# Banded attention into a squared-ReLU MLP: the last quarter of W1 in two column halves, the first loads in another order, one group's gate moved

## The chip, the cores and the metric

One core of a Trainium2 chip runs the whole program; seven cores are not used. The metric is the device time of one execution in microseconds (us), lower is better. The time before is the median of three runs. A profile is one further execution, recorded by the hardware; its span is the stretch from the first to the last recorded instruction, a little less than the device time of that same execution.

The engines go by short names: PE (matrix multiply), PEld (its weight load), DVE (vector), ACT (scalar, activation), POOL (GpSimd), SP (sync). Each runs its own instructions strictly in the order in which they were written into its stream; an instruction that waits on a semaphore holds up everything behind it on that engine. Transfers are started by POOL, SP and ACT and are carried out by 16 shared DMA engines.

## The reference

```python
# q, k, v: [8 batches, 8 heads, 576 tokens, 64], float32
scores = (q @ k.T) / sqrt(64);  only |query - key| <= 32 is kept
attn   = softmax(scores);       x = attn @ v
x      = x as [8*576 = 4608 tokens, 8*64 = 512]
h      = x @ w_in               # w_in  (W1): 512 x 2048
g      = relu(h) ** 2
out    = g @ w_out              # w_out (W2): 2048 x 512
```

## The kernel before, in words

**Groups.** The 4608 tokens are cut into 24 groups G of 192 query tokens, three to a batch (b, g = G // 3, G % 3). A group has two key windows of 128 keys, w = 0 ("A") and w = 1 ("B"). The program names its steps, and the texts below use the same names:

- `turnk`, `turnq` (L485): for the first two batches, G < 6, PE transposes the rows of k and q into `kt` and `qt`; the result is evicted from PSUM by DVE (k, L516) or ACT (q, L513). Later groups are turned by DMA transposes from SP (L524).
- S (L565) scores of a group, X (L586 for group 0, L589 for the rest) the exponential on ACT, M (L594) the band mask on DVE. For group 0 the mask is added in PSUM as a bias (L548), so it has no M.
- P (L613, L617, L622) attention times v, with a column of ones that gives the row sums; R (L641) the reciprocal, N (L644) the normalisation into `xa` (64 tokens) and `xb` (128 tokens), Z (L650) a memset of part of the PSUM tile between PA and PB.
- T and XT: x is transposed into `xt`, by PE and evictions for G < 3 (L666, L671, L696, L701; L675, L685, L688, L713), by DMA transposes from SP afterwards (L717, L720).
- A (`mm1`, L737): x times W1, in blocks of 192, later 256 and 512 tokens. At 192 tokens one piece covers two of the sixteen 128-column strips d of W1, that is eight matmuls; the eight pieces of the first block are A0.0, A0.2, ... A0.14. Then Relu on ACT (L743) and the square on DVE (L746) into `gt`.
- B (`mm2`, L757): 128 tokens times W2, four matmuls for each quarter of W2, then an eviction on ACT (L767) and a store. The last 128 tokens go through `mm2_last` (L782).

**Loads.** k, q and v of the first groups, W1 and W2 are loaded by POOL (the transfers convert float32 to bfloat16). k and q of group 0 come instead through SP as float32 into the output buffer `oe` (`load_hw`, L407) and are cast by ACT and DVE (L414, L417). For groups 1 to 5, `load_pair` (L426) loads k or q into a pair buffer `PR[t][G % NPR]`, and a DVE copy (L429) sorts the pairs into `raw`; with three such buffers groups 4 and 5 use those of groups 1 and 2 again, so their POOL transfer waits for the earlier copy. W1 comes in four quarters of 512 columns (`load_w1`, L456), each with a semaphore of its own; piece A.d waits for quarter d // 4. W2 comes in four quarters of 512 rows (L461). `copy_v` (L450) copies 64 rows of one v tile to the next instead of loading them twice.

**Order.** The table `OPENING` gives the order of the first transfers: entry number n gets the priority `K + n` with K = -100, and POOL issues in this order. All other work has a key that grows with the group or the token block. `Prog.rec` notes every operation with what it reads and writes, an estimated duration and its key. `Prog.schedule` is a list planner: whenever an engine is free in the planner's own clock, it takes the ready operation with the least key. It has a small model of the DMA queues (`move`, `slack`, `LANDQ`), so the planned landing of a load decides where its consumers stand in each engine's stream. `Prog.emit` writes the streams in the planned order, with semaphore waits for what is not ordered already. The planner's times have no effect on the chip except through this order. Where PE would stand idle before the second transpose of group 0's `xb`, the planner fills the gap with matmuls on zeros ("idle", L322) that nothing reads.

**The gate.** Loads from group 6 on (`load_qk`, L394, and `load_v`, L443) carry an extra dependency from `gate(G)`: for G below `GFAR` the A piece or score that was recorded last at that point (`self.moe`), from `GFAR` on the step PB of group G - 3. POOL waits for it before it issues the load. The key of these loads is 3G - 13 - 9, from `GFAR` on 3G - 13 - 8.5.

Of the kernel before, what the change touches and what calls it, by code (L numbers as in the profile page):

```python
# [22 lines left out]
LEAD = 13.0  # L23
LAG = 9.0
AHEAD = 9.0
GFAR = 9
GATE = 'P{}B'
GD = 3
GK = 8.5
# [3 lines left out]
HMOVE = 27  # L33
PMOVE = 20
WMOVE = 81
VMOVE = 14.5
TISS = 1340
TMOVE = 15
NVR = 24
VKEY = 10.0  # L40
TSLACK = 3500
XSLACK = 2500
LSLACK = 3000
NCLR = 1
LANDQ = 2000
PQ = 100
VCS = 6
NDUP = 1
NPR = 3
LSLACK1 = 1000  # L50
HOLD = {}
KMIN = 0.5
HOLDT = 26000
KSPL = 0
XTD = 1
NSPLIT = 3
HWB = 150
# [8 lines left out]
VSET = (-9.8, -6.8)  # L66
ESPLIT = 0
IOTA = -1
OPENING = [("k", 1), ("w1", 0), ("v", 0, 0), ("v", 1, 1), ("q", 1), ("v", 0, 1), ("q", 2), ("k", 2), ("v", 1, 0), ("w1", 1),
           ("w1", 2), ("w1", 3), ("q", 5), ("v", 2, 0), ("v", 2, 1), ("w2", 1), ("k", 3), ("v", 3, 0), ("q", 3), ("w2", 0), ("w2",  # L70
           2), ("k", 4), ("v", 3, 1), ("q", 4), ("v", 5, 0), ("v", 5, 1), ("w2", 3), ("hq", 0), ("k", 5), ("v", 4, 0), ("v", 4, 1),
           ("hk", 0)]
WARM = 40000
LAST = ((0, 256), (256, 384), (384, 512))
KC = ((0, 224), (224, 192), (416, 160))
# [204 lines left out]
class Gen:  # L280
# [5 lines left out]
    def alloc(self):  # L286
# [24 lines left out]
        self.OEB = sb("oe", [128, 4, 512], F32)  # L311
        self.PR = {t: [sb(f"{t}pair{i}", [128, 1024], BF16) for i in range(NPR)] for t in "qk"}
        self.BIAS = [sb(f"bias{i}", [128, 128], BF16) for i in range(4)]
# [67 lines left out]
    def gate(self, G):  # L381
        if G < 6:
            return None
        return self.p.named[GATE.format(G - GD)] if G >= GFAR else self.moe

# [33 lines left out]
    def load_pair(self, t, b, g, key):  # L419
# [3 lines left out]
        G = 3 * b + g  # L423
        pr, raw = self.PR[t][G % NPR], self.RAW[t][G % NRAW]
        s = (self.q if t == "q" else self.k)[b][:, t0:t0 + n, :].rearrange("h (p r) d -> p h (r d)", r=2)
# [8 lines left out]
    def load_v(self, b, g, key, js=(0, 1)):  # L434
        G = 3 * b + g
        vt = self.V[G % NV]
        for j in js:
            k0 = 192 * g - 32 + 128 * j
            lo, hi = max(k0, 0), min(k0 + 128, S_)
            if g and j == 0 and G < NVR:  # L440
# [3 lines left out]
                vt[lo - k0:hi - k0, j, :, 0:64], self.v[b, :, lo:hi, :].rearrange("h p d -> p h d")),  # L444
                writes=[("v", G % NV, j)], dma=(f"v{G % NV}{j}", G), key=key, dur=500 + 3 * n, move=(n // 2, VMOVE),
                name=f"v{b}{g}{j}", after=self.gate(3 * b + g), slack=LSLACK if b > 1 else LSLACK1 * b)
# [4 lines left out]
                   reads=[("v", (G - 1) % NV, 1)], writes=[("vl", G % NV)], key=key + VKEY, dur=300, name=f"vc{G}",  # L451
                   after=self.moe if G >= VCS else None)

    def load_w1(self, d, key):
        src = self.w_in[:, 512 * d:512 * d + 512].rearrange("(f p) c -> p f c", p=128)
        self.p.rec("POOL", lambda e: e.dma_start(self.W1[:, :, 512 * d:512 * d + 512], src),  # L456
                   writes=[("w1", d)], dma=(f"w1{d}", 0), key=key, dur=770, move=(32, WMOVE), name=f"w1{d}")

    def load_w2(self, d, key):
        src = self.w_out[512 * d:512 * d + 512, :].rearrange("(k p) c -> p k c", p=128)  # L460
        self.p.rec("POOL", lambda e: e.dma_start(self.W2[:, 4 * d:4 * d + 4, :], src),  # L461
                   writes=[("w2", d)], dma=(f"w2{d}", 0), key=key, dur=770, move=(32, WMOVE), name=f"w2{d}")

# [8 lines left out]
    def turn_pe(self, t, b, g, key):  # L472
# [32 lines left out]
        w = (t + "t", b % 2, g)  # L505
        if t == "k" and G == 0 and KSPL:
            for x, (c0, c1) in enumerate(((0, KSPL), (KSPL, h))):
# [144 lines left out]
    def xturn(self, G):  # L652
# [4 lines left out]
        if G < NXT:  # L657
# [48 lines left out]
            if two:  # L706
                for x, (c0, c1) in enumerate(((0, 64), (64, 192))):
# [10 lines left out]
                   reads=[("xa", G % 3)], writes=wr[:1], dma=(f"xa{G % 3}", G), key=key - 0.5 + XKEY[0], dur=TISS, move=(16, TMOVE), name=f"T{G}a",  # L718
                   slack=XSLACK)
        self.p.rec("SP", lambda e: e.dma_start(self.XT[:, :, r + 64:r + 192], xb[:], transpose=True),  # L720
                   reads=[("xb", G % 3)], writes=wr[1:], dma=(f"xb{G % 3}", G), key=key - 0.5 + XKEY[1], dur=TISS, move=(32, TMOVE), name=f"T{G}b", slack=XSLACK)

    def mm1(self, t0, n, ds, key):
        k = self.k1
        self.k1 += 1
        ht, rt, gt = self.HT[k % 2], self.RT[k % 4], self.GT
        r = t0 % RING
        c = n * len(ds)  # L730
        d0 = ds[0]
        steps = [(t0 // 64 + x) % (RING // 64) for x in range(n // 64)]

        def f(e):
            for x, d in enumerate(ds):
                for ft in range(4):
                    mm = e.matmul(ht[:, n * x:n * x + n], self.W1[:, ft, 128 * d:128 * d + 128], self.XT[:, ft, r:r + n],  # L737
                                  start=(ft == 0), stop=(ft == 3))
            return mm

        self.moe = self.p.rec("PE", f, reads=[("xt", s) for s in steps] + [(("xt", s), 1) for s in steps if t0 < 192 and XTD] + [("w1", d0 // 4)], writes=[f"ht{k % 2}"], key=key,
                   dur=4 * len(ds) * max(n / 2.4 + 2.5, 33), name=f"A{t0}.{d0}")
        self.p.rec("ACT", lambda e: e.activation(rt[:, 0:c], ht[:, 0:c], ACTF.Relu), reads=[f"ht{k % 2}"],  # L743
                   writes=[("rt", k % 4)], key=key, dur=act(c), name=f"r{t0}.{d0}")
        rr = rt[:, 0:c].rearrange("p (d t) -> p d t", d=len(ds))
        self.p.rec("DVE", lambda e: e.tensor_tensor(gt[:, d0:d0 + len(ds), r:r + n], rr, rr, ALU.mult),  # L746
                   reads=[("rt", k % 4)], writes=[("gt", s, d) for s in steps for d in ds], key=key, dur=dve(c),
                   name=f"g{t0}.{d0}")
# [50 lines left out]
    def build(self):  # L799
        p = self.p  # L800
        self.k1 = 0
        self.moe = None
        K = -100.0
        self.setup_idle()
        self.setup_iota(K + IOTA)
        self.setup_id(K)
        self.setup_mask(2, K + 1)
        self.setup_bias(2, K + 1.1)
        self.setup_mask(1, K + 2)
        self.setup_bias(1, K + 2.1)  # L810
        self.setup_k(0, K + 0.5)
        self.setup_v(0, K + 1.5)
        self.setup_v(1, VSET[0])
        self.setup_v(2, VSET[1])
        self.setup_mask(0, MKEY[0])
        self.setup_mask(3, MKEY[1])
        for i in range(3, NV):
            self.setup_v(i, -9)
        self.setup_k(1, -9)
        for n, it in enumerate(self.opening()):  # L820
            kd, a = it[0], it[1:]
            key = K + n
            if kd == "w1":
                self.load_w1(a[0], key)
            elif kd == "w2":
                self.load_w2(a[0], key)
            elif kd == "v":
                self.load_v(*divmod(a[0], 3), key, a[1:])
            elif kd[0] == "h":
                self.load_hw(kd[1], a[0], key)  # L830
            else:
                self.load_pair(kd, *divmod(a[0], 3), key)
        for g in (1, 2, 4, 5):
            self.copy_v(g, K + 7 if g < 3 else 3 * g - LEAD - AHEAD)
        todo = []

        def at(key, f, *a):
            todo.append((key, len(todo), f, a))

        for G in range(NG):  # L840
            b, g = divmod(G, 3)
            if b > 1:
                key = 3 * G - LEAD - (GK if G >= GFAR else AHEAD)
                for t in "kq":
                    at(key, self.load_pair if G < NPAIR else self.load_qk, t, b, g, key)
                at(key, self.load_v, b, g, key)
                if g and G < NVR:
                    key = 3 * G - LEAD - 0.5 if G >= VCS else key
                    at(key + 0.01, self.copy_v, G, key - VKEY if G >= VCS else key)
            for t in "kq":  # L850
                key = 3 * G - LEAD - (0.6 if b < NTURN else TDKEY)
                at(key, self.turn_pe if b < NTURN else self.turn_dma, t, b, g, key)
            for ws in ((0,), (1,)) if G < NSPLIT else ((0, 1),):
                at(3 * G - LEAD + 0.3 * ws[0], self.scores, G, ws)
            for w in range(2):
                at(3 * G - LEAD + 0.3 * w + 0.1, self.pv, G, w)
            at(3 * G - LEAD + 0.5, self.xturn, G)
        t0 = 0
        while t0 < NTOK:
            n = FIRST[t0] if t0 in FIRST else 192 if t0 < 768 else 256 if t0 < T512 else 512  # L860
            m = min(512 // n, 4)
            for d in range(0, 16, m):
                key = t0 / 64 + d / 16 * n / 64
                at(key, self.mm1, t0, n, list(range(d, d + m)), key)
            t0 += n
        at(500, self.mm2_last, NBLK - 1, 500)
        for u in range(NBLK - 1):
            for seg in range(4):
                at(2 * u + LAG + seg * 0.5, self.mm2, u, seg, 2 * u + LAG + seg * 0.5)
        for key, _, f, a in sorted(todo, key=lambda x: x[:2]):  # L870
            f(*a)
        p.schedule()
        with self.nc.Block():
            dsems, dcount = p.emit()
            for s in dsems:
                if s[0] == "o":
                    self.nc.sync.wait_ge(dsems[s], dcount[s])
# [35 lines left out]
```

## Time and profile before

| | us |
|---|---|
| median of 3 runs (lowest to highest) | 302.03 (301.92 to 302.29) |
| profiled execution, device time | 301.87 |
| its span | 299.9 |
| PE busy in the span | 291.9 (97%) |
| DVE, ACT, POOL busy | 167.2, 160.3, 107.1 |
| first piece of x times W1 starts | 17.46 |
| last of the eight pieces of the first block starts to run, with the one before it | 24.11 |
| stores left after the last matmul | 297.58 to 299.9 |

The span can be read in three parts. Until 17.46 us PE does the transposes, scores and P V of the first groups, with zero matmuls between them. From there to about 297.6 us it is busy nearly without a gap. Then the last stores land. The granted PE clock is 1.00 throughout. The DMA engines are busy from 3 us to about 230 us.

### The profile page before, as it was taken

The page shows a single profiled execution, that of the slowest core. Times are in us where ns is not written, and L with a number is a line of the kernel's source. Part 1 is how long each engine was busy: PE and PEld are TensorE (multiplying, and loading weights), DVE is VectorE, ACT ScalarE, POOL GpSimd, SP SyncE. Part 2 cuts the span into 40 slices and gives each one's busy share as a digit, 9 for nine tenths or more (in the row PEclk, how much of TensorE's full clock was granted, in tenths as well). Part 3 has the DMA queues.
Part 4 walks back from the last instruction along what each step waited for, and adds up shares of the span by engine and source line. Part 5 has one row for each costly group of instructions (what it writes and reads, how often), then busy time and mean ns, then how long its engine had stood idle before and what let it go on. Part 6 is the DMA issues. An engine that isn't in the chain of part 4 may idle for free.

```text
span 299.9 us, 6209 instructions
## 1 busy us (share of the span) xinstructions
PE 291.9 (97%) x2394; PEld 171.8 (57%) x2431; DVE 167.2 (56%) x385; ACT 160.3 (53%) x250; POOL 107.1 (36%) x143
## 2 busy tenths in 40 slices
PE   7899999999999999999999999999999999999996
PEld 3578866848677767664544454444544444444445
DVE  6898775737674767563656666665666632222100
ACT  3497834836467656750765476536744643443312
POOL 8993336503544354455256335533500000000000
PEclk9999999999999999999999999999999999999999
DMA  9999999997999999999999999999992120100112
GB/s 169 176 206 184 196 177 174 169 176 137 164 169 165 95 162 146 155 138 186 180 168 131 114 166 156 125 149 156 154 128 70 55 61 35 37 35 35 38 70 105
DMA packets 160636, 39.83 MB, mean 133 GB/s; under 512 B 149984, under 2 KB 156128, under 8 KB 160608
## 3 DMA queue, kind: packets, MB, share of 16 engines
q0 software_dynamic: 106016, 17.93, 89.3%
q1 hardware_dynamic: 49264, 12.14, 28.5%
q10 hardware_dynamic: 5328, 9.37, 9.1%
q8 instruction: 19, 0.31, 0.5%
q14 instruction: 9, 0.07, 0.1%
HBM read 36.70 MB, written 9.44 MB: 154 GB/s over the span
## 4 chain that ended last, share of the span: by engine, by line
PE 90%; DMA 5%; POOL 3%; issue 1%; ACT 0%; POOLq 0%; ACTq 0%
PE ht L737 41%; PE outp L757 40%; DMA w<-in_moe_w_in_dram 5%; PE at L622 4%; PE at L565 4%; POOL v L443 1%; POOL w L456 1%; PE at L485 1%; PE ht L782 1%; PE outp L782 1%; POOL kpair L426 1%; POOL qpair L426 1%; ACT rt L743 0%; ACT oe L792 0%; POOL dif L325 0%
## 5 line engine op out<-in xcount | busy, mean ns | idle before, releaser
L737 PE MATMUL ht<-xt,w 128*128 128x256 bf16 (+2 forms) x885 | 140.0, 302 | 1.3 <-DMA w<-in_moe_w_in_dram 0.5
L757 PE MATMUL outp<-w,gt 128*128 128x512 bf16 x536 | 133.0, 379 | 1.3
L743 ACT ACTIVATE rt<-ht 128x512 bf16<-128x512 f32 (+1 forms) x152 | 85.9, 578 | 87.1 <-PE ht L737 85.1
L737 PEld LDWEIGHTS ht<-xt,w 128*128 128x128 bf16 x896 | 81.3, 98 | 43.8 <-ACT rt L743 0.6
L746 DVE TENSOR_TENSOR gt<-rt 128x512 bf16<-128x512 bf16 (+1 forms) x152 | 61.5, 408 | 61.6 <-ACT rt L743 60.0
L757 PEld LDWEIGHTS outp<-w,gt 128*128 128x128 bf16 x560 | 51.9, 98 | 54.1 <-ACT oe L767 1.0
L394 POOL DMA_DIRECT2D kraw<-in_k_dram x36 | 27.7, 778 | 107.3 <-PE at L622 56.8
L589 ACT ACTIVATE e<-at 128x1024 bf16<-128x1024 f32 x46 | 44.8, 1021 | 8.7 <-PE at L565 8.4
L594 DVE TENSOR_TENSOR pt<-e,mask 128x1024 bf16<-128x1024 bf16 x46 | 31.8, 691 | 29.0 <-ACT e L589 28.9
L443 POOL DMA_DIRECT2D v<-in_v_dram x48 | 38.2, 809 | 0.0
L767 ACT ACTIVATE oe<-outp 128x512 f32<-128x512 f32 x35 | 21.1, 604 | 29.6 <-PE outp L757 29.6
L394 POOL DMA_DIRECT2D qraw<-in_q_dram x36 | 27.7, 778 | 0.0
L622 PEld LDWEIGHTS at<-v,pt 128*128 128x128 bf16 x384 | 18.3, 98 | 9.9 <-DMA v<-in_v_dram 0.6
L622 PE MATMUL at<-v,pt 128*128 128x65 bf16 x384 | 20.1, 194 | 0.5 <-ACT pt L586 0.5
L644 DVE TENSOR_TENSOR xa<-at,rs 64x512 bf16<-64x512 f32 x24 | 16.7, 695 | 0.9
L644 DVE TENSOR_TENSOR xb<-at,rs 128x512 bf16<-128x512 f32 x24 | 16.5, 689 | 0.7
L565 PEld LDWEIGHTS at<-qt,kt 64*128 64x128 bf16 x384 | 10.8, 94 | 8.7 <-issue 7.1
L565 PE MATMUL at<-qt,kt 64*128 64x128 bf16 x384 | 15.2, 217 | 0.2
L641 DVE RECIPROCAL rs<-at 64x8 f32<-64x8 f32 (+1 forms) x48 | 10.0, 209 | 9.1 <-PE at L622 7.7
L650 DVE MEMSET at<- 64x520 f32 x23 | 11.3, 492 | 3.5 <-DVE xa L644 2.6
L450 DVE COPY v<-v 64x512 bf16<-64x512 bf16 x16 | 5.9, 372 | 5.1 <-PE ht L737 2.9
L789 DVE COPY oe<-ht 128x128 f32<-128x128 f32 x1 | 0.3, 292 | 14.5 <-PE ht L782 14.5
(67 smaller groups left out, 83.2 us busy)
## 6 DMA issues: line engine op xcount, KB each, us to landing
out_dram<-oe ACTq DMA_DIRECT2D x35, 256.0 KB, 3.2
qraw<-in_q_dram POOLq DMA_DIRECT2D x36, 96.0 KB, 5.8
w<-in_moe_w_in_dram POOLq DMA_DIRECT2D x4, 512.0 KB, 10.7
v<-in_v_dram POOLq DMA_DIRECT2D x16, 128.0 KB, 6.6
w<-in_moe_w_out_dram POOLq DMA_DIRECT2D x4, 512.0 KB, 18.8
v<-in_v_dram POOLq DMA_DIRECT2D x16, 96.0 KB, 7.0
kraw<-in_k_dram POOLq DMA_DIRECT2D x12, 112.0 KB, 4.6
kraw<-in_k_dram POOLq DMA_DIRECT2D x12, 96.0 KB, 4.9
```

Of the source, the lines that this page charges most:

```text
L394: self.p.rec("POOL", lambda e, j=j: e.dma_start(raw[0:h, j, :].rearrange("p (h d) -> p h d", h=8), s[:, j]), writes=[("raw", t, G % NRAW, ...
L443: self.p.rec("POOL", lambda e, j=j, lo=lo, hi=hi, k0=k0: e.dma_start(vt[lo - k0:hi - k0, j, :, 0:64], self.v[b, :, lo:hi, :].rearrange("h ...
L565: mm = e.matmul(sc[:, 512 * par + 128 * j:512 * par + 128 * j + 128], kt[r:r + 64, j, k0:k0 + 128], q, start=G >= NBIAS, stop=True, skip_g ...
L589: self.p.rec("ACT", lambda e, e_=e_, sc=sc: e.activation(e_[:], sc, ACTF.Exp, scale=0.125), reads=tags[w], writes=[("e", n % 2)], key=key, ...
L594: self.p.rec("DVE", lambda e, pt=pt, ee=ee, mb=mb: e.tensor_tensor(pt[:], ee, mb, ALU.mult), reads=[("e", n % 2), ("mask", mi)], writes=[( ...
L622: mm = e.matmul(avp[:, c:c + 65], pt[:, 4 * (h % 2) + h // 2, :], vt[:, w, h, 0:65], start=(w == 0 and y == 0), stop=True, skip_group_chec ...
L644: self.p.rec("DVE", lambda e: e.tensor_tensor(x[r0:128, :].rearrange("p (x y c) -> p x y c", x=2, y=4), av[:, :, :, 0:64], rb, ALU.mult), ...
L737: mm = e.matmul(ht[:, n * x:n * x + n], self.W1[:, ft, 128 * d:128 * d + 128], self.XT[:, ft, r:r + n], start=(ft == 0), stop=(ft == 3))
L743: self.p.rec("ACT", lambda e: e.activation(rt[:, 0:c], ht[:, 0:c], ACTF.Relu), reads=[f"ht{k % 2}"], writes=[("rt", k % 4)], key=key, dur= ...
L746: self.p.rec("DVE", lambda e: e.tensor_tensor(gt[:, d0:d0 + len(ds), r:r + n], rr, rr, ALU.mult), reads=[("rt", k % 4)], writes=[("gt", s, ...
L757: mm = e.matmul(op[:], gt[:, d, r:r + 128], self.W2[:, d, :], start=(d == 0), stop=(d == 15))
L767: self.p.rec("ACT", lambda e: e.activation(oe, op[:], ACTF.Copy), reads=[f"outp{u % 2}"], writes=[("oe", u % 4)], key=key, dur=act(512), n ...
```

## The change

1. `load_w1` takes an optional half. The last quarter of W1 is loaded as two transfers of 256 columns, each with its own semaphore; a piece of `mm1` waits only for the half that it reads. The other three quarters are loaded as before, under two names.
2. `OPENING` has a new order. q of group 2 is POOL's first transfer, in place of k of group 1; v of group 0 comes next; the first quarter of W1 moves from second to seventh place; the order behind W1 changes too.
3. `KSPL` goes from 0 to 48: the eviction of group 0's transposed k (L516) is done in two instructions, the first with keys 0 to 95, so that the scores of window A of group 0 wait only for the first. The code for this is in the kernel already.
4. `NPR` goes from 3 to 4: a fourth pair buffer each for k and q.
5. `GFAR` goes from 9 to 10: group 9's loads are gated by `self.moe` and have the key 5 in place of 5.5.
6. `XSLACK` goes from 2500 to 3000: the planner counts 0.5 us more until a DMA transpose of x has landed.

```diff
-GFAR = 9
+GFAR = 10
 WMOVE = 81
+WHALF = 43
-XSLACK = 2500
+XSLACK = 3000
-NPR = 3
+NPR = 4
-KSPL = 0
+KSPL = 48
-OPENING = [("k", 1), ("w1", 0), ("v", 0, 0), ("v", 1, 1), ("q", 1), ("v", 0, 1), ("q", 2), ("k", 2), ("v", 1, 0), ("w1", 1),
-           ("w1", 2), ("w1", 3), ("q", 5), ("v", 2, 0), ("v", 2, 1), ("w2", 1), ("k", 3), ("v", 3, 0), ("q", 3), ("w2", 0), ("w2",
-           2), ("k", 4), ("v", 3, 1), ("q", 4), ("v", 5, 0), ("v", 5, 1), ("w2", 3), ("hq", 0), ("k", 5), ("v", 4, 0), ("v", 4, 1),
-           ("hk", 0)]
+OPENING = [("q", 2), ("hq", 0), ("v", 0, 0), ("v", 0, 1), ("hk", 0), ("v", 1, 1), ("k", 1), ("q", 1), ("w1", 0), ("k", 2), ("v",
+           1, 0), ("w1", 1), ("w1", 2), ("w1", 3, 0), ("w1", 3, 1), ("v", 2, 0), ("v", 2, 1), ("w2", 0), ("k", 3), ("q", 3), ("v",
+           3, 1), ("q", 5), ("w2", 1), ("v", 5, 1), ("v", 3, 0), ("w2", 2), ("k", 4), ("q", 4), ("w2", 3), ("v", 4, 1), ("k", 5),
+           ("v", 4, 0), ("v", 5, 0)]
-    def load_w1(self, d, key):
-        src = self.w_in[:, 512 * d:512 * d + 512].rearrange("(f p) c -> p f c", p=128)
-        self.p.rec("POOL", lambda e: e.dma_start(self.W1[:, :, 512 * d:512 * d + 512], src),
-                   writes=[("w1", d)], dma=(f"w1{d}", 0), key=key, dur=770, move=(32, WMOVE), name=f"w1{d}")
+    def load_w1(self, d, key, half=None):
+        c, n = (512 * d, 512) if half is None else (512 * d + 256 * half, 256)
+        src = self.w_in[:, c:c + n].rearrange("(f p) c -> p f c", p=128)
+        self.p.rec("POOL", lambda e: e.dma_start(self.W1[:, :, c:c + n], src),
+                   writes=[("w1", d, x) for x in ((0, 1) if half is None else (half,))], dma=(f"w1{c}", 0), key=key, dur=770,
+                   move=(32, WMOVE if half is None else WHALF), name=f"w1{d}" + ("" if half is None else f".{half}"))
...
-        self.moe = self.p.rec("PE", f, reads=[...] + [("w1", d0 // 4)], ...
+        self.moe = self.p.rec("PE", f, reads=[...] + [("w1", d0 // 4, x) for x in sorted({d // 2 % 2 for d in ds})], ...
...
             if kd == "w1":
-                self.load_w1(a[0], key)
+                self.load_w1(a[0], key, *a[1:])
```

More of the change, by code (lines that the diff above doesn't have):

```diff
@@ L739, in f @@
             return mm
-        self.moe = self.p.rec("PE", f, reads=[("xt", s) for s in steps] + [(("xt", s), 1) for s in steps if t0 < 192 and XTD] + [("w1", d0 // 4)], writes=[f"ht{k % 2}"], key=key,
+        self.moe = self.p.rec("PE", f, reads=[("xt", s) for s in steps] + [(("xt", s), 1) for s in steps if t0 < 192 and XTD] + [("w1", d0 // 4, x) for x in sorted({d // 2 % 2 for d in ds})], writes=[f"ht{k % 2}"], key=key,
                    dur=4 * len(ds) * max(n / 2.4 + 2.5, 33), name=f"A{t0}.{d0}")
```

## The prediction

> **What bounds the kernel now.** I read the page's chain of work that ended last first, then the same chain in order of time, then PE's waits and PE's timeline of the first 26 us, then the other engines and the landings there.
>
> ```profile
> PE 90%; DMA 5%; POOL 3%; issue 1%; ACT 0%; POOLq 0%; ACTq 0%
> ```
> ```profile
> 10.19 13.79 DMA w<-in_moe_w_in_dram
> 23.98 0.14 issue
> 24.11 1.48 PE ht L737 x16
> ```
>
> From 24.11 on the chain is PE. What starts it is the last quarter of W1: issued at 10.19, landed at 23.98. PE's waits of at least 0.2 us behind the first piece of x times W1 (17.46) are this one of 0.5 and two of 0.2. Windows of 50 us between 50 and 250 show PE busy for 49.53 to 49.63 us. So PE has a fixed amount of work after the opening, and the change can only move the moment from which it is packed, or open a hole later.
>
> ```profile
> 13.78 0.51 PE L485 MATMUL ht<-ident,qraw 96*128 96x96 bf16 x8 [0.17 <-DVE qraw L429]
> 14.13 0.42 PE L613 MATMUL at<-v,pt 128*128 128x65 bf16 x8
> 15.42 0.40 PE L565 MATMUL at<-qt,kt 64*128 64x128 bf16 x8
> 17.14 0.40 PE L565 MATMUL at<-qt,kt 64*128 64x128 bf16 x8
> 17.46 0.83 PE L737 MATMUL ht<-xt,w 128*128 128x192 bf16 x8
> ...
> 24.11 1.48 PE L737 MATMUL ht<-xt,w 128*128 128x192 bf16 x16 [0.47 <-DMA w<-in_moe_w_in_dram]
> 25.43 0.42 PE L622 MATMUL at<-v,pt 128*128 128x65 bf16 x8
> ```
>
> The columns are start, duration, what, and in brackets the idle time before and who ended it. The second window of group 0 (PB, 14.13) stands behind turnq1; scores S1A and S1B run at 15.42 and 17.14. The wait of 0.47 stands before A0.12 and A0.14, which need the last quarter; they end at 24.11 + 1.48 = 25.59. That is my reference point.
>
> Landings (issue plus time to landing): k1 7.3, W1.0 9.8, v00 10.5, v11 11.5, q1 12.4, v01 13.3, q2 14.4, k2 15.5, v10 15.7, W1.1 18.2, W1.2 21.3, W1.3 24.0. POOL had issued all of these by 11, so the order of issue and the width of the path set them, and the steps between them are prices: a W1 quarter 2.5 to 3.1, a q or k pair 0.9 to 1.1, a v tile 0.2 to 1.0.
>
> **The last quarter.** The twelve transfers up to W1.3 are the same ones as before, in another order, so the last byte lands where it did, about 24.0. The split adds one issue on POOL (0.77, L456; POOL runs ahead of the landings by 13, so nobody waits for it) and one more transfer. The trace has no half of a quarter. Nearest rows for the extra transfer: v10 landed 0.2 behind k2, so at most about 0.2 more; the quarters' steps of 2.5 to 3.1 leave 0.3 to gain. I take 0.1, the row of the small transfer being nearer: last half at 24.1, first half about 1.4 before it, 22.7. PE started 0.14 after the landing. Now one piece instead of two stands behind it, 1.48 / 2 = 0.74. End of the first block: 24.1 + 0.14 + 0.74 = 24.98, against 25.59: **-0.6**, with -1.0 and -0.5 as the bounds by landing alone. It holds only if PE has finished all else by 24.24.
>
> The Trainium skill, page "DMA: Bandwidth & Descriptors", section "Anatomy of one DMA — SWDGE (gpsimd) path", gives each such transfer a fixed cost of about 2.0 us and, in "Measured (HBM→SBUF, 128 partitions, SWDGE, issued from GpSimd)", advises batches of at least 1 MiB, which speaks against splitting a quarter that reads 1 MB. If that fixed cost added up in the queue, the sum would be 2 us worse; by the rows here transfers land 0.2 to 1.1 apart, so the trace does not bear it out for transfers queued behind each other.
>
> **The opening, in the new order.** Summing the steps from the first landing at 7.3: q2 7.3, v00 8.0, v01 8.9, v11 9.9, k1 10.9, q1 11.8, W1.0 14.3, k2 15.3, v10 15.6, W1.1 18.2, W1.2 21.2. The planner's keys and due times I use for the order on each engine only; every duration is a row.
>
> - *The split eviction.* Before, L516 took 1.15 from 8.36 and X0A ran at 10.01. L516 took 0.87, 1.02, 1.15 for 640, 768, 896 columns, so 384 columns take about 0.6: S0A could be ready 0.5 earlier. But q2, now first, is turned in between: its copy takes k1's place on DVE (8.02), turnq2 ends near 9.0, and its eviction on ACT (1.03, as the row of q1 at 14.33) stands ahead of X0A until 10.0. I take a gain of **0** for the split; bounds 0 and 0.5.
> - *PB of group 0.* v01 lands at 8.9, not 13.3, and q1's turn no longer stands before PB. X0B ends at 11.95 as before; turnk1 (copy after k1 at 10.9, DVE busy with a v copy and the masks until 11.2) is ahead of it, so PB starts near 12.4 and ends 13.35, 1.7 earlier.
> - *DVE and ACT give part back.* Ahead of N0B on DVE stand now k1's eviction (1.02) and q1's copy (0.42): N0B at 14.3 to 15.0, against 15.43 to 16.12. Then q1's eviction on ACT (15.2 to 16.2) stands before the second XT: x of group 0 is ready near 16.6. S1A waits for that same eviction: 16.3, 0.9 later than before. turnk2 follows, and A0.0 starts near 17.0, 0.45 earlier. S1B (0.33 of PE) is not yet done by then, as it was before: the lead in finished PE work is 0.1 to 0.3.
> - *17 to 24.* Before, PE worked 6.1 us from 17.46 without a wait, to 23.6. All of that is still to do, plus S1B and A0.12: 17.0 + 6.1 + 0.33 + 0.74 = 24.2. This meets the 24.24 above, with nothing to spare. Any wait here (P1B behind Z and M, both near 21.2) comes straight off the gain.
>
> ```profile
> 23.68 0.81 ACT L713 ACTIVATE xt<-at 128x768 bf16<-128x768 bf16 x1
> ```
>
> XT1 ended at 24.49; behind it wait P2A (25.43) and the next block's first piece (25.85). With S1A 0.9 late and ACT nearly full (1.78 to 2.00 of each 2 us between 16 and 24), XT1 may end up to 0.9 later, 25.4. The packed PE wants it at 24.98, but turns and scores of group 2 were its last users before, and X2B keeps only 0.9 of that delay at most; I take 24.9, no wait.
>
> **Behind the opening.** v31 landed at 39.3 and now follows q3 near 31, so P3B and the transpose of `xb` (issued at 42.16) come sooner; v30 moves from 29.9 to about 36.1, against P3A at 36.77; k4 and q4 move from 38.0 and 40.0 to about 40 and 41, against their turns at 42.51. Each is covered by 0.2 to 2 us, for which blocks already in `xt` and W2 work fill PE; without cover PE waits the difference. The fourth pair buffer removes a wait of q5 on POOL (before, q5 went out at 15.7 behind q3, although listed earlier): nothing waits for q5 until after 50, so 0. Group 9's gate moves from PB of group 6 (71.38; POOL issued at 72.24) to its scores (65.35): the loads go some 6 earlier, among SP's transposes for group 8, of which the last, issued near 70.4, took 2.8. Transposes that overlapped loads took up to 8.0 (issued at 53.7), so 78.4 at worst, and S8 runs at 81.58: 0. `XSLACK` only makes the planner place A pieces later: 0, since these show no wait before.
>
> **Sum:** -0.6 in the opening, 0 behind it. Against the profiled execution, 301.87 - 0.6 = 301.3; that one lies 0.16 below the median, so against the median 302.03 - 0.6 = **301.4**. A difference of 0.2% (0.6 us) is about what a measurement of this kernel can tell from no change.
>
> **Rivals.**
>
> 1. *A larger gain, 300.7.* If DVE's and ACT's give-back is smaller than I think, XT1 comes before the last half, and one piece of the next block (0.74) fits in front of it: -0.6 - 0.74 = -1.35. For it: 4.35 us of zero matmuls between 6.08 and 15.3 show that the room is there. Against it: the two evictions ahead of XT and S1A.
> 2. *The gain is spent between 17 and 24, 301.8.* PE waits 0.4 on P1B or S2A; of 0.6 then 0.2 stays. For it: DVE 1.76 to 2.00 of 2 us in those windows. Against: other pieces stand close by in the order.
> 3. *Slower, 302.7.* The later S1A drives the chain X1A, S1B, X1B, S2A, X2A, X2B, XT1 on ACT. It decides once XT1 ends later than 25.85, that is 1.36 behind before; from there PE loses one for one, as P2A and the next block wait for it. At a slip of 2.0, 0.65: 302.7. For it: PE order is fixed, and each wait adds to the 0.9. Against: q2's turn is already done, which frees 1.04 of ACT at 17.04.
> 4. *The halves cost a transfer each, 303.5.* The second half is not carried beside the first; then it lands later by the shortest issue to landing seen here, 2.4 (a store at 72): 26.4 + 0.14 + 0.74 = 27.3, +1.7, of which some 0.2 is filled. This is what the Trainium skill's fixed cost (page and section above) would amount to.
>
> **Chances.** Forecast 0.48 (own range 301.0 to 301.8), rival 1 0.18, rival 2 0.17, rival 3 0.14, rival 4 0.03. Of the forecast's cases 0.30 lie more than 0.2% below, 0.18 inside, since an early landing and a filled PE add up to -1.0. Faster: 0.30 + 0.18 = 0.48. Same: 0.18 + 0.17 = 0.35. Slower: 0.14 + 0.03 = 0.17. The range holds the forecast, rivals 1 and 2 and the start of rival 3: 300.6 to 302.5.
>
> **What would show it.** Right: the wait of L737 on W1 is gone or below 0.2, the first block ends near 25.0, A0.0 starts near 17.0, PB of group 0 near 12.4, X0A still near 10.0, q1's eviction just before XT, group 9's loads near 66 and no new wait of PE behind 26. Wrong: last half later than 24.3, PE idle between 17 and 24, XT1 beyond 25.85, or a wait for v30, k4 or a transpose.

## The result and the profile after

The changed kernel takes 302.62 us (median of 20 runs, 302.14 to 303.24) against 302.11 (20 runs, 301.58 to 302.90) for the kernel before on the same chip: ratio 1.0016, 95% interval 1.0009 to 1.0023. It is slower by half a microsecond, where 0.6 us less was forecast. A second series gave 1.0018 (1.0010 to 1.0027). The profiled execution took 303.0 (span 300.9), at the upper end of the runs; that of the kernel before took 301.87, near the lower end of its own. So the pair of profiles shows twice the median difference, and a second profile of the changed kernel (302.31, span 300.2) is read beside it.

The page's chain of work that ended last is PE's even more than before:

```profile
PE 91%; DMA 4%; POOL 3%; DVE 1%; issue 0%; ACT 0%; POOLq 0%; DVEq 0%
```

PE's timeline of the changed kernel in the opening (start, duration, what, count, idle time before and who ended it):

```profile
12.02 0.42 PE L616 MATMUL at<-v,pt 128*128 128x65 bf16 x8
...
13.72 0.51 PE L488 MATMUL ht<-ident,qraw 96*128 96x96 bf16 x8 [0.21 <-DVE qraw L430]
...
15.44 0.40 PE L568 MATMUL at<-qt,kt 64*128 64x128 bf16 x8 [0.34 <-DVE xb L647]
...
16.01 0.51 PE L488 MATMUL ht<-ident,qraw 96*128 96x96 bf16 x8
...
17.68 0.83 PE L740 MATMUL ht<-xt,w 128*128 128x192 bf16 x8
...
22.14 1.49 PE L740 MATMUL ht<-xt,w 128*128 128x192 bf16 x16 [0.27 <-DMA w<-in_moe_w_in_dram]
...
24.02 1.76 PE L740 MATMUL ht<-xt,w 128*128 128x192 bf16 x16
25.62 0.42 PE L625 MATMUL at<-v,pt 128*128 128x65 bf16 x8
```

PB of group 0 (12.02) comes 2.1 earlier than before, yet S1A (15.44) and the first piece of x times W1 (17.68) do not. The row of S1A names N0B, which S1A does not read; q of group 1, which it does read, was evicted on ACT by 15.30, 0.05 before N0B ended. The old wait of 0.47 for W1's last quarter is gone, but a wait of 0.27 for the third quarter stands at 22.14, and inside the group at 24.02 there is a hole that the chain in order of time shows:

```profile
24.85 0.12 issue
24.97 0.82 PE ht L740 x8
```

A0.14 starts at 24.97, 0.14 behind the landing of the last half at 24.83. The first block ends at 25.79, against 25.59 before. Of the loss of 1.07 us in span, 0.19 is there when the second block starts (25.88, 25.69 before); the rest comes later, as these figures from the PE timelines show (us; "between" is the last column but one minus the second):

| kernel | first piece | second block starts | last matmul starts | between |
|---|---|---|---|---|
| before | 17.46 | 25.69 | 297.36 | 271.67 |
| changed, first profile | 17.68 | 25.88 | 298.40 | 272.52 |
| changed, second profile | 17.34 | 25.63 | 297.65 | 272.02 |

PE's work in that stretch is the same; what grows is small holes (0.14 at W2's last quarter at 44.44 in the first profile, none there in the second). The largest in the first profile is 0.36 us, at PB of group 9, of which the profile counts 0.20 as idle. First PE, then DVE of the changed kernel:

```profile
94.46 1.91 PE L740 MATMUL ht<-xt,w 128*128 128x256 bf16 x16
96.57 0.43 PE L625 MATMUL at<-v,pt 128*128 128x65 bf16 x8 [0.20 <-DVE at L653]
```
```profile
92.75 0.61 DVE L451 COPY v<-v 64x512 bf16<-64x512 bf16 x1 [0.17 <-PE ht L740]
...
94.44 0.21 DVE L644 RECIPROCAL rs<-at 64x8 f32<-64x8 f32 x1
...
95.14 0.69 DVE L647 TENSOR_TENSOR xa<-at,rs 64x512 bf16<-64x512 f32 x1
96.02 0.49 DVE L653 MEMSET at<- 64x520 f32 x1 [0.18 <-DVE xa L647]
```

PB waits for the memset Z, which ends at 96.51. Between PA and PB stand one piece of W2 and two of W1, as in the kernel before, where this PB runs at 100.96 without a hole. There Z ends at 100.68:

```profile
100.19 0.49 DVE L650 MEMSET at<- 64x520 f32 x1 [0.18 <-DVE xa L644]
```

What differs is DVE's stream. In the changed kernel a copy of v (L451) stands between the two masks of group 9 and pushes the second mask, R, N and Z back; the kernel before has no such copy between two masks behind 50 us. In the first profile the copy took 0.61. In the second it took 0.29, and the same place has no hole (Z runs at 95.25, PB at 95.83), but one of 0.16 stands at 156.74, behind the copy at 153.1, again between two masks. The kernel before has no hole at P V behind 26 us.

### The profile page after: what moved, and what is told of

Its sections match the earlier page's. It is cut to its first block, busy times and chain, and to the rows that moved or that the text cites. A ratio compares the mean times of both kernels' runs of the same rounds, so it can differ in the third digit from the quotient of the medians.

```text
span 300.9 us, 6252 instructions
## 1 busy us (share of the span) xinstructions
PE 294.0 (98%) x2429; PEld 170.7 (57%) x2429; DVE 165.2 (55%) x386; ACT 161.0 (54%) x250; POOL 108.0 (36%) x144
## 4 chain that ended last, share of the span: by engine, by line
PE 91%; DMA 4%; POOL 3%; DVE 1%; issue 0%; ACT 0%; POOLq 0%; DVEq 0%
PE ht L740 41%; PE outp L760 40%; DMA w<-in_moe_w_in_dram 4%; PE at L568 4%; PE at L625 4%; POOL v L444 1%; PE at L488 1%; PE ht L785 1%; PE outp L785 1%; POOL qpair L427 1%; POOL kpair L427 1%; POOL w L458 0%; DVE gt L749 0%; DVE xa L647 0%; DVE pt L597 0%
## 5 line engine op out<-in xcount | busy, mean ns | idle before, releaser
L760 PE MATMUL outp<-w,gt 128*128 128x512 bf16 x560 | 137.1, 379 | 0.0
L323 PE MATMUL outp<-zz 128*128 128x512 bf16 x23 | 7.2, 445 | 1.2 <-DVE zz L317 1.2
```

Source lines behind the costliest of these rows:

```text
L760: mm = e.matmul(op[:], gt[:, d, r:r + 128], self.W2[:, d, :], start=(d == 0), stop=(d == 15))
```

## The experiments

All ratios are against the kernel before on the same chip, with 95% intervals. Landings are the time of issue plus the time to landing in the view of DMA issues.

**The changed kernel again**

```diff
(no edit)
```

> The changed kernel once more, unaltered. Theory A (transfers): with the small v transfers early on POOL's queue everything behind lands later, so k of group 0 lands again near 7.1 us (6.6 before), W1's second quarter near 19.5 (18.2 before) and the last half near 24.8 (24.0 before). Rival B (one execution's chance): these landings fall back to 6.6, 18.2 and 24.0, and the first piece of x times W1 starts before 17.4. Both expect 0.1 to 0.25% above the kernel before, and the hole of 0.36 us on PE near 96 again.

302.60, ratio 1.0018 (1.0010 to 1.0027). k of group 0 landed at 6.46, so its lateness in the first profile (7.16) was chance; with it the first piece moved from 17.68 to 17.34. W1's second quarter and last half were late again (19.08 and 24.58). The hole at 96 did not come back. Theory A held for W1 in this profile, not for the first loads.

**The split alone**

```diff
-           ("w1", 2), ("w1", 3), ("q", 5), ...
+           ("w1", 2), ("w1", 3, 0), ("w1", 3, 1), ("q", 5), ...
```

> The kernel before with its last quarter of W1 split in two halves, and nothing else. Theory A: the old order keeps the old landings, last half at 24.0 to 24.2, the wait of 0.47 for W1 goes, the first block ends near 25.0 instead of 25.6, and the time falls by 0.3 to 0.6 us. Rival: each transfer costs something of its own, or other work stands in the way, and the time stays within 0.2 us of before.

302.76, ratio 1.0019 (1.0010 to 1.0028). The landings are those forecast: first half 22.70, last 24.04, and the second block starts at 25.17, 0.52 earlier. But the kernel is slower. The extra issue on POOL let q of group 5 go out ahead of q of group 3 (a pair buffer was free in time), the planner ordered the work behind it anew, and PE met W2's last quarter, which landed at 43.88:

```profile
42.38 1.02 PE L760 MATMUL outp<-w,gt 128*128 128x512 bf16 x4
43.93 1.04 PE L760 MATMUL outp<-w,gt 128*128 128x512 bf16 x4 [0.52 <-DMA w<-in_moe_w_out_dram]
```

From the second block's start to the last matmul it takes 273.24, 1.57 more than before.

**All edits but the new order of loads**

```diff
 (the changed kernel's constants)
+OPENING = (the order of the kernel before, W1's last quarter in one piece)
```

> The changed kernel with the old order of the first loads (the halves of W1's last quarter in place of the quarter). Theory A: landings as in the kernel before (k of group 0 at 6.6, W1.1 at 18.2, last half at 24.1), so the loss goes: 0 to 0.6 us below before. Rival C (the loss is in the order of the later work, from the gate and the planner's later landings): no better than the changed kernel, +0.4 to +0.6 us, with a hole on PE near 96.

The kernel that ran had the last quarter whole, not in halves as the expectation says. 303.05, ratio 1.0030 (1.0019 to 1.0041). W1.1 landed at 18.48 and the last quarter at 24.11, and it is still slow: "between" is 273.19, with a hole of 0.35 at 94.67, again PB of group 9. The copy of v between that group's masks took 0.60 here. In the four other profiles in which it stands there (the second look at the changed kernel, and the runs below with the allowance for x, with three pair buffers and with x ahead) it took 0.29, and none of them has a hole at that PB; these six are the profiles with `GFAR` at 10. So the loss is not the order of loads alone; this is the rival's outcome. Why the copy is sometimes twice as long is open.

**The new order of loads alone**

```diff
-OPENING = (old)
+OPENING = (new, with ("w1", 3) in one piece)
```

> The kernel before with the new order of the first loads alone (W1's last quarter in one piece). Theory A: landings of W1 late by 0.5 to 0.9 us as in the changed kernel, A0.12 starts near 24.9, the first block ends near 26.4, and the time is 0.6 to 1.0 us above before. Rival C: W1 lands as before and the time stays within 0.2 us of it.

304.53, ratio 1.0081 (1.0068 to 1.0095). W1's last quarter landed at 23.80, so it was not the landing: P V of group 2 stood at once behind the eviction of x of group 1, and PE waited for that. The waits of PE behind 17 us:

```profile
PE at L625 <- ACT xt L716: 1.2, 1, 1.2
PE ht L740 <- DMA xt<-xb: 0.4, 1, 0.4
PE ht L740 <- ACT qt L516: 0.3, 1, 0.3
```

Both theories missed this. What an order of loads is worth goes through the order of work that the planner makes of it.

**The new order and the split, nothing else**

```diff
+OPENING = (new)
 GFAR = 9; XSLACK = 2500; NPR = 3; KSPL = 0
```

> The kernel before with the new order of the first loads and the split, nothing else. Theory E (new order and split together put the last half late): it lands at 24.5 to 24.9 as in the two looks at the changed kernel. Rival (that was chance, or came from the other edits): 23.8 to 24.1, as with either part alone. The first block ends 0.14 + 0.74 behind that landing or, if P V of group 2 stands in front, up to 1 us later; time 0.3 to 1.0 us above before.

302.77, ratio 1.0024 (1.0013 to 1.0036). Last half at 24.01: theory E fell. Here too P V of group 2 waits for XT1 (0.3 counted), and the second block starts at 26.03.

**The planner's allowance for x put back**

```diff
-XSLACK = 3000
+XSLACK = 2500
```

> The changed kernel with the planner's allowance for the transposes of x put back from 3000 to 2500. Theory F (the later half of the loss, 0.3 us behind 25 us in the second look at the changed kernel, comes from where the work stands in PE's stream behind 60 us): the opening is the same, the small holes near 96 and 156 us shrink, and the time falls 0.2 to 0.5 us below the changed kernel, to 302.1 to 302.4. Rival (the loss is in the transfers of the opening): 302.5 to 302.7, the same as the changed kernel.

303.21, ratio 1.0033 (1.0021 to 1.0044): no better than the changed kernel, against theory F, and above the 302.7 of its rival too. The opening is the same (second block 25.57, last half 24.52); a hole of 0.72 opened ahead of 68.46.

**W2's last quarter earlier**

```diff
-... ("v", 3, 1), ("q", 4), ("v", 5, 0), ("v", 5, 1), ("w2", 3), ...
+... ("v", 3, 1), ("w2", 3), ("q", 4), ("v", 5, 0), ("v", 5, 1), ...
```

> The split-only kernel with one entry of the order moved: the last quarter of W2 goes out ahead of q of group 4 instead of four transfers later. Theory D (a lead won at W1 is lost at the next landing, W2's last quarter at 43.9, where PE stood 0.68 us): W2's last quarter lands near 41.8, the hole near 43 goes, and the time falls 0.4 to 0.7 us below the split-only kernel, to about 302.1 to 302.4. Rival (the lead is lost anyway, at the x of group 3 or at P V of group 4): a hole of the same size opens before 54 us and the time stays within 0.2 us of the split-only kernel, 302.8.

On top of the split alone: 302.22, ratio 1.0005 (0.9996 to 1.0013), 0.5 below the split alone. The quarter landed at 41.77 and the hole at 43 is gone. "Between" is still 272.93, with holes of 0.23 at 32.02, 0.14 at 51.88, 0.25 at 52.39 and 0.21 at 158. Theory D held in its main point, the rival in part.

**Another order behind W1, in two forms**

```diff
+OPENING = [... ("w1", 3, 1), ("v", 2, 0), ("v", 4, 0), ("v", 2, 1), ("k", 3), ("q", 3), ("w2", 0), ("v", 3, 0), ("w2", 1),
+           ("v", 5, 0), ("q", 4), ("w2", 2), ("k", 4), ("v", 3, 1), ("hk", 0), ("w2", 3), ("v", 5, 1), ("k", 5), ("hq", 0), ("v", 4, 1), ("q", 5)]
```

> The split-only kernel with all transfers behind W1 in another order: W2's first two quarters earlier, q and v of group 5 later. Theory D: first block ends 0.5 earlier than in the kernel before, W2's last quarter lands 1.5 us or more ahead of its use, no hole on PE over 0.3 us between 25 and 60, and the time is 0.3 to 0.7 us below before. Rival (what is won in the opening goes in small holes behind 60 us, in any new order of the work): within 0.2 us of before, with holes of 0.1 to 0.4 us on PE at P V between 60 and 200.

302.59, ratio 1.0009 (1.0001 to 1.0018). This order also put k of group 0 ahead of q on SP, which the expectation does not say; the first piece started at 17.99. "Between" is 271.73, as good as before, but this is the profile of the fastest of the twelve executions (301.70; the median is 302.59), so what the others lost stays open. In this one little lead was won in the opening: the last half landed at 24.46, and the second block starts at 25.58, 0.11 earlier than before.

The second form exchanges ("hq", 0) and ("hk", 0):

> The split with the other order behind W1, now with q of group 0 ahead of k on SP as in the kernel before (the earlier form had them the other way round and its first piece of x times W1 started 0.53 late, at 17.99). Theory D: first piece near 17.45, second block near 25.15, W2's last quarter lands near 42.4 just ahead of its use, time 0.3 to 0.6 us below before. Rival (holes in any new order): 302.2 to 302.6.

308.84, ratio 1.0216 (1.0194 to 1.0239). First piece at 17.35, but ACT's issue of one store took 5.26 us, where the others of this kernel take 0.34 to 0.36, and everything behind it on ACT waited. ACT's timeline, PE's, and a window of the kernel (length, then busy time of PE, PEld, DVE, ACT and POOL, the granted clock, the DMA share and GB/s):

```profile
44.57 5.26 ACTq L769 DMA_DIRECT2D out_dram<-oe  x1
```
```profile
51.04 0.62 PE L565 MATMUL at<-qt,kt 64*128 64x128 bf16 x16 [4.27 <-ACT qt L513]
51.98 4.07 PE L757 MATMUL outp<-w,gt 128*128 128x512 bf16 x11 [0.31 <-issue]
```
```profile
53.00:55.00 2.00, 2.00 (x7) 0.62 (x5) 1.38 (x2) 0.94 (x2) 2.00 (x3) 0.50 1.09 171
```

So this order could not be judged by its loads. Why the issue took that long is open.

**Three pair buffers in the changed kernel**

```diff
-NPR = 4
+NPR = 3
```

> The changed kernel with three pair buffers in place of four; every engine's order is that of the changed kernel. Theory: the fourth buffer costs and brings nothing; W1's last half lands at 24.5 or later as in three looks with four buffers, time 302.5 to 302.8. Rival (the fourth buffer is what puts the last half late): it lands at 24.0 to 24.1, the second block starts 0.4 earlier, time 0.2 to 0.4 us below the changed kernel.

302.46, ratio 1.0010 (1.0001 to 1.0019); the interval overlaps that of the changed kernel. The last half landed at 24.28 and the second block started at 25.25, 0.44 earlier than before, yet "between" is 272.35, 0.68 more. So even where the opening gains, this order of the work gives it back. For the fourth buffer nothing is resolved.

**x of group 0 ahead of the exponential of group 1**

```diff
         self.moe = self.p.rec("PE", f, reads=rd, writes=[t for w in ws for t in tags[w]], key=key, dur=190 + 235 * len(ws),
-                              name=f"S{G}{'AB'[ws[-1]]}")
+                              name=f"S{G}{'AB'[ws[-1]]}", after=self.p.idle_end if G == 1 and ws[0] == 0 else None)
```

> The changed kernel with S1A made to wait for the last transpose of group 0's x, so that on ACT the eviction of x runs ahead of the exponential of group 1. Theory H (in the changed kernel the first piece of x times W1 was held by q1's eviction and X1A on ACT, not by P V of group 0; and an earlier first piece buys nothing, since W1's last half ends the block): first piece at 16.6 to 16.9 in place of 17.34, second block no earlier than 25.5, time 0 to 0.5 us above the changed kernel. Rival (the attention chain bounds the opening): the first piece stays near 17.3, or the second block starts 0.4 earlier and the time falls by as much.

302.92, ratio 1.0029 (1.0017 to 1.0041). The first piece starts at 16.94, 0.40 earlier than in the second profile of the changed kernel, and PE then waits 0.81 us before A0.8 for W1's third quarter; the profile counts 0.6 of it:

```profile
PE ht L740 <- DMA w<-in_moe_w_in_dram: 0.6, 1, 0.6
```

The second block starts at 26.04. An earlier first piece buys nothing, as theory H has it, but not for its reasons. The second XT ran at 16.48, against 16.46 in the second profile of the changed kernel: q of group 2's eviction (15.59 to 16.62) took the place of X1A ahead of it, and the first piece gained because S1B no longer stands before it. Nor does W1's last half end the block: it landed at 24.06, the block's last piece ran at 24.63, and then PE waited for XT1, which ended at 25.64, with P2A at 25.79.

**The split with every engine's order kept**

```diff
+WHALF = 40.5
-                   writes=[...], dma=(f"w1{c}", 0), key=key, dur=770,
-                   move=(32, WMOVE if half is None else WHALF), name=...)
+                   writes=[...], dma=(f"w1{c}", 0), key=key, dur=770 if half is None else 385,
+                   move=(32, WMOVE if half is None else WHALF), name=..., slack=1296 if half == 0 else 0)
```

The old order of loads, the old constants, and numbers for the halves by which the planner arrives at the streams of the kernel before.

> The kernel before with the split alone, and with the planner's numbers for the halves set so that every engine's order stays that of the kernel before (POOL only has the one more issue). Theory G (the split is worth what was forecast, and the new order of the work eats it): first block ends 0.4 to 0.6 us earlier, the second block starts near 25.2; PE may wait up to 0.2 at W2's last quarter near 43.7; time 0.3 to 0.6 us below before. Rival (the lead has no room behind the opening even in the old order): PE gives the lead back in holes at W2 or at the x of group 3 before 60 us, time within 0.15 us of before.

302.06, ratio 1.0001 (0.9992 to 1.0010). The halves landed at 22.53 and 24.10, and the second block starts at 25.07, **0.62 earlier** than before. By 48.5 it is all gone, and PE is 0.27 behind; it stays so from P V to P V to the end, so PE's order is indeed the same. PE, then DVE, of this kernel:

```profile
42.63 1.03 PE L760 MATMUL outp<-w,gt 128*128 128x512 bf16 x4
43.91 1.04 PE L760 MATMUL outp<-w,gt 128*128 128x512 bf16 x4 [0.25 <-DMA w<-in_moe_w_out_dram]
...
48.44 0.41 PE L625 MATMUL at<-v,pt 128*128 128x65 bf16 x8 [0.25 <-DVE pt L597]
```
```profile
47.24 0.33 DVE L451 COPY v<-v 64x512 bf16<-64x512 bf16 x1 [1.83 <-DMA v<-in_v_dram]
47.60 1.29 DVE L597 TENSOR_TENSOR pt<-e,mask 128x1024 bf16<-128x1024 bf16 x2
```

and of the kernel before at the same place:

```profile
43.19 1.89 PE L757 MATMUL outp<-w,gt 128*128 128x512 bf16 x8
45.01 0.62 PE L565 MATMUL at<-qt,kt 64*128 64x128 bf16 x16
45.57 2.76 PE L757 MATMUL outp<-w,gt 128*128 128x512 bf16 x11
48.17 0.42 PE L622 MATMUL at<-v,pt 128*128 128x65 bf16 x8
```

W2's last quarter landed at 43.86 here and at 43.67 before. Before, the four matmuls that need it start at 43.19 + 4 x 0.216 = 44.05, 0.4 behind the landing; with the lead of 0.56 that PE has there it stands, with 0.41 from the last matmul's end to the next start. Then the copy of v for group 5 (L451) waits on DVE for v of group 4, with the masks of group 4 behind it and PA of group 4 behind these: another 0.41. That landing was 47.22 here and 46.57 before. Here PA starts 0.15 behind the end of its mask (48.29); before, that mask ended at 47.63, so PA, at 48.17, had some 0.4 to spare. The rival is right about the time, and the place is these two landings. But part of the loss is that both came later than before, by 0.19 and 0.65. With the landings of before, these rows leave a lead of some 0.3 (an estimate: 0.56 less 0.41, plus 0.19). The split alone had that v at 46.04, so the split need not make it late; one profile of each cannot tell this from chance.

**q of group 5 last, with and without the split**

```diff
+        for x, y in (("q12", "v111"), ("cq12", "N4B")):
+            self.ops.remove(self.named[x])
+            self.ops.insert(self.ops.index(self.named[y]) + 1, self.named[x])
```

At the end of `schedule`: q of group 5 (192 KB, used behind 50 us) goes out behind v of group 4, and its copy on DVE moves behind group 4's work. All other orders stay.

> The kernel before with the split, and q of group 5 loaded last of the first transfers (its copy on DVE moved behind group 4's); all other orders as in the kernel before. Theory I (the second bound is the landings from 43 to 48 us): W2's last quarter lands near 42.8, v of group 4 near 46.2, the holes of 0.41 at 43.3 and 47.8 go to below 0.1, PE keeps the 0.6, and the time is 0.4 to 0.7 us below before, 301.5 to 301.8. Rival (PE loses the lead at any rate, at x of group 3 or later): another hole of 0.3 to 0.6 opens between 43 and 60 us and the time stays within 0.15 us of before.

> The kernel before with q of group 5 loaded last and its copy moved, without the split. Theory I: landings behind 31 us are 1 us earlier, but PE is still held by W1's last quarter at 24.0 and has no other wait: time within 0.15 us of before. Rival (the late transfers alone held the kernel): 0.3 to 0.6 us below before.

With the split: **301.65, ratio 0.9981 (0.9973 to 0.9990)**, 0.56 us below the kernel before, about 1.0 below the changed one, which ran on another chip. Without: 301.93, ratio 0.9991 (0.9982 to 1.0000). With the split, W2's last quarter landed at 42.35 and v of group 4 at 45.97, the second block starts at 25.04, and both holes are closed. PE of the kernel with both:

```profile
42.61 1.89 PE L763 MATMUL outp<-w,gt 128*128 128x512 bf16 x8
44.43 0.62 PE L571 MATMUL at<-qt,kt 64*128 64x128 bf16 x16
44.98 2.76 PE L763 MATMUL outp<-w,gt 128*128 128x512 bf16 x11
47.58 0.42 PE L628 MATMUL at<-v,pt 128*128 128x65 bf16 x8
...
67.39 1.03 PE L743 MATMUL ht<-xt,w 128*128 128x256 bf16 x8 [0.18 <-DMA xt<-xa]
```

Row for row 0.6 ahead of the kernel before. A third landing takes half of it at 67.39, a transpose of x (a hole of 0.34, of which 0.18 is counted). From there on PE is 0.25 ahead. So a gain of the forecast's size is there with the two edits together. The split's own share, on top of the late q, is the 0.28 between the two medians. That the late q brings the other 0.28 by itself was not expected; its interval touches 1, and its profile does not show where it would come from: W2's last quarter landed at 42.35, v of group 4 at 46.60 as before and not 1 us earlier, and the last matmul starts at 297.51, against 297.36 before.

## Why the prediction was wrong

**The last quarter: right in itself.** Last half at 24.1, first block 0.6 shorter: with the orders kept the halves landed at 22.53 and 24.10, and the second block came 0.62 earlier. The fixed cost per transfer in the Trainium skill, page "DMA: Bandwidth & Descriptors", section "Anatomy of one DMA — SWDGE (gpsimd) path", did not add up in the queue: the two halves landed 1.57 us apart there, and the last one 0.12 behind the whole quarter of the kernel before. Rival 4 falls.

**The last half in the changed kernel: a term mis-sized.** It was put at 24.1 and landed at 24.83 and 24.58. That turned the lead of 0.6 into -0.19 and +0.06 at the start of the second block, so of the 1.1 us between forecast and result some 0.5 to 0.8 are lost here. In the other kernels with the new order and the halves it landed at 24.01, 24.06, 24.28 and 24.52. In those with the old order through W1.3 it landed at 24.04, 24.07, 24.10 and 24.11, but at 24.46 and 24.61 in the two forms of the other order behind W1. The same transfers in the same order thus landed anywhere from 24.01 to 24.83, where the forecast left 0.1 and at most 0.2. The bytes moved by 24 us on POOL's queue are much the same (3450 KB and 3470 KB in the two profiles of the changed kernel, 3496 KB before, in 1000 bytes, summed over packets); but when the last half lands, 3616 KB and 3584 KB have been moved, against 3492 KB at the last quarter's landing before. So later transfers were ahead while some packets of W1 were behind. Why is open.

**The opening's order: wrong in detail.** q of group 2 is not turned before X0A: it shares the bank `ht1` with q of group 1 and is recorded behind it, so it runs at 16.01. PB was early, as forecast (12.02 against 12.4). N0B came at 14.68 (forecast 14.3) and S1A at 15.44 (16.3). So S1A did not come late as forecast, but as early as before (15.42). The first piece was forecast at 17.0 and came at 17.68 and 17.34. The second XT had ended at 17.18 and 16.84 by then; PE was still at the turn of k of group 2, which had waited for its copy on DVE (16.95 and 16.61), and at S1B, both ahead of the first piece in its stream. That leaves PB's 2.1 us without effect. The run with x ahead shows that this is not what held the time.

**"0 behind it": the step that failed.** It took covers of 0.2 to 2 us for enough, priced the loads that move, and put the new order of every engine's work at nothing. In the changed kernel "between" is 0.35 and 0.85 more. Its largest hole and that at 156.74 stand at PB behind a copy of v that the new order puts between two masks on DVE. That place costs 0.36 where the copy took 0.61, and nothing where it took 0.29. "Between" grew in every kernel with new streams, by 0.06 to 1.57 us (the one with the long issue left out), through holes at P V, at W2 and at x.

Covers of 0.4 were not enough either. W2's last quarter and v of group 4, each with some 0.4, were not priced, and a lead of 0.6 has to pass both. With the orders kept it did not pass (302.06, with both landings later than before). The changed kernel had no such lead, so there these landings cost 0.14 in one profile and nothing in the other. Which of the six edits makes which part of the new order was not settled. The copy between group 9's masks, and that group's P V some 4 to 7 us earlier in PE's stream than before, are seen in all six profiles with `GFAR` at 10 and in none with 9, but `GFAR` and `KSPL` were not tried alone.

**The rivals.** Rival 3 named a number near the result (302.7), but not the way: XT1 ended at 25.03, well before its point of 25.85. It was near by chance. Its wait of P2A for XT1 is real in other kernels with the new order: with x ahead, and with the new order and the split alone, XT1 ended at 25.64 and PE stood, although that is ahead of 25.85, since PE was there earlier than before. Rival 1 fell: no time was won. Rival 2 was right in that the gain is spent, but not on P1B or S2A: PE waited for W1's third quarter at 22.14 (0.27 counted), and the last half landed late. Rival 4's price of 2.4 was not the shortest seen: a store at 298.0 landed in 1.57. Group 9's loads went out at 66.78 (forecast near 66), and no wait for them shows; the 2.8 read for the transpose issued near 70.4 is the median of two, and it took 2.32 itself.

## What to carry to other kernels

Where one engine is busy throughout, a lead won at one landing is worth what the next landings leave of it: list every landing with its cover, not only those that move. Where a planner makes the order, an edit is two edits; force the old order to see what the edit itself is worth, then look at what the new order costs, on the engines that are not the bottleneck too: here a copy on DVE made the largest hole on PE.

## What was not expected of the hardware

One issue of a store on ACT's queue took 5.26 us in the kernel of 308.84 us. It was the first store of the kernel. The first store's issue took 2.72 us in the other form of that order and 2.83 with x ahead, where PE shows no wait for it, and at most 0.40 in all other profiles. In the kernel of 308.84 us it cost more than its wait: PE stood still for more than 4 us, and from 53 to 55 us the granted clock was 0.50; the eleven recorded W2 matmuls from 51.98 took 4.07, against 2.76 for eleven in the kernel before. The Trainium skill, page "TensorE: Matmul & The Clock Gate", section "What's actually happening", has the clock halve after an idle window of some 3.4 us; this trace agrees with it (0.50 behind 4.27 us without a matmul).
